# A few small products ahead of each pair of blocks in layer two

## The chip, the core and the metric

The kernel is one program on one core of a Trainium2 chip. The metric is device time in microseconds (us). Five engines have their own queues and run side by side: TensorE (PE, matrix products into PSUM, with the loading of weights shown apart as PEld), VectorE (DVE), ScalarE (ACT), GpSimd (POOL) and SyncE (SP, which issues the DMAs). They wait for one another through semaphores.

## What is computed

```python
def reference(**kwargs):
    attn_out = _attn_ref(**attn_kwargs)            # random-feature attention, 4 x 8 heads x 576 x 64
    x = attn_out.transpose(0, 2, 1, 3).reshape(B * S, H * D)     # 2304 tokens x 512
    x = _moe_ref(x=x, **moe_kwargs)                # layer one: h = x @ w_in; max(0.01 h, h) @ w_out
    return _moe2_ref(x=x, **moe2_kwargs)           # layer two, below

def _moe2_ref(x, w_in, w_out):                     # 512 -> 2048 -> 512
    h = x @ w_in
    relu6 = np.clip(h + 3.0, 0.0, 6.0)
    g = h * relu6 / 6.0
    return (g @ w_out).astype(np.float32)
```

All of it is in fp32. The change stands in the first product of layer two.

## The kernel before

**Number formats.** The large products of both layers hold each fp32 operand as two parts, high and low, of type fp32r, and make three products for one: high by high, low by high, high by low. One such product is one weight load and one matmul record in the trace. The products of the attention are plain fp32; each of them shows as two matmul records (the list of nine products in `K_unit` stands in the trace as 18 records of line L781). All records print "f32".

**Stages.** The 2304 tokens are cut into five groups of 512, 256, 512, 512 and 512 (`GN`). Attention for the next group runs between the products of layer one on the current group. Layer two follows, in the order of groups 0, 2, 3, 4, 1 (`ORDER2`); its first products already stand among the last of layer one.

**Layer two.** For a group of 512 tokens, `moe2` calls `Hpair(i)` for i = 0 to 7, one call for each pair of blocks of 128 hidden columns. It forms the pair's 2x2 block product by seven products of blocks (a Strassen form) instead of eight. `prod` issues one of the seven: six matmuls of 128x128 weights by 256 columns (line L1152, 42 matmuls a pair, 1344 in all for the 32 pairs of the four large groups). The results go into three regions: `R[0]` is the first half of PSUM bank `p`, `R[1]` and `R[2]` are the halves of bank `q`. The first product of a pair writes `R[0]` with `start` set at its first matmul, which clears it. The weights come by DMA into tiles (`fetch`, seen as `late_w<-in` or `third_w<-in`). Afterwards ACT and DVE make the activation, and `down` makes the output products (line L1057, also 128x256). The group of 256 tokens goes through `Hsingle`, which the change does not touch.

**Order.** A planner (`Graph.run`) lists all operations with costs and due times when the program is built, and writes each engine's queue in the order that it finds. A product's cost to the planner is the number in its `g.op(("pe", cost, mm))` call.

**Constants.** `ident` is a 128x128 identity, `ones` 128x128 of ones, both fp32; `zero` is 128x128 of zeros in fp32r. All are written once at the start of the program.

**Lines of the rows below.** L491 to L493 are the three products of `mm3` (layer one, 512 or 256 columns); L781 the product of keys and values in `K_unit`, 66 columns; L931 the transposes in `Q_unit`; L962 its numerator, with 64 stationary columns, written into either half of the PSUM partitions.

Of the kernel before, what the change touches and what calls it, by code (L numbers as in the profile page):

```python
# [325 lines left out]
def c_dve(n):  # L326
    return n / 0.96 + 69.0
# [6 lines left out]
def c_act(n, psum=False, ap=False):  # L334
    return n / 1.2 + (51.0 if psum else 93.0) + (93.0 if ap else 0.0)
# [6 lines left out]
def c_mm(n):  # L342
    return 114.0 if n == 256 else max(112.0, n / PACE)
# [7 lines left out]
def attn_moe_kernel(ctx: ExitStack, tc: tile.TileContext, qT, kT, qn, kn, v1, om2, w1i, w1o, w2i, w2o, out):  # L351
# [4 lines left out]
    nc = tc.nc  # L356
# [12 lines left out]
    def sb(name, shape, dt=F32, pool=const):  # L369
        return pool.tile(shape, dt, name=name)  # L370
# [91 lines left out]
    ident = sb("ident", [128, 128])  # L462
    wn = sb("wn", [128, 128])
    ones = sb("ones", [128, 128])
    zero = sb("zero", [128, 128], F32R)
# [4 lines left out]
    def Ps(use):  # L470
        return Buf("ps", use)


    def copy_alts(dst, src, n, psum=False):

        dve = ("dve", c_dve(n) if psum else c_dve2(n), lambda: nc.vector.tensor_copy(dst(), src()))
        return [("act", c_act(n, psum), lambda: nc.scalar.copy(dst(), src())), dve if psum else dve + (True,)]  # L477
# [9 lines left out]
    def two(b):  # L487
        return b.tiles[0].rearrange("p (k n) -> p k n", k=2)
# [154 lines left out]
    def fetch(b, kind, i, part, due, cols=slice(0, 512), to=0):  # L643
        d, done = late_w[kind, i, part]
        n = cols.stop - cols.start
        g.op([("sp", c_dma(128 * n * 8), lambda: nc.sync.dma_start(
            b.tiles[2].rearrange("p (h c) -> p h c", h=2)[:, :, to:to + n].bitcast(F32), d[:, :, cols].bitcast(F32)))],
             rd=[done, *ready.values()] if kind == "in" else [done], wr=[(b, to)], due=due)
        return b
# [464 lines left out]
    def moe2(grp, T):  # L1114
# [19 lines left out]
        def Hpair(i):  # L1134


            t0 = T + UP * i
            d = t0 - 8e3
            c = [Buf("w", line="c") for _ in range(4)]
            for k in range(4):  # L1140
                fetch(c[k], "in", i, k, d + UP * 0.1 * k, slice(0, 256) if k == 2 else slice(0, 512))
            p, q = Ps("H"), Ps("H")
            R = [lambda: p.tiles[0][:, 0:256], lambda: q.tiles[0][:, 0:256], lambda: q.tiles[0][:, 256:512]]
            bank = [(p, 0), (q, 0), (q, 1)]

            def prod(r, a, off, b, at, start):
                def mm():
                    for k in range(2):
                        w = [c[a].tiles[h][:, off + k * 128:off + k * 128 + 128] for h in range(2)]
                        m = [b.tiles[h][:, k * 256:k * 256 + 256] for h in range(2)]  # L1150
                        for n, (x, y) in enumerate(((0, 0), (1, 0), (0, 1))):
                            nc.tensor.matmul(R[r](), lhsT=w[x], rhs=m[y], start=start and k == n == 0, stop=k == 1 and n == 2,  # L1152
                                             skip_group_check=True)
                g.op([("pe", 6 * c_mm(256), mm)], rd=[c[a], b], wr=[bank[r]], due=t0 + UP * at, lag=APART if r == 0 and not start else 0.0)

            s, h0, h1 = Buf("u", line="s"), Buf("u", line="h"), Buf("u", line="h")
            hold = lambda i: s.tiles[0][:, i * 256:i * 256 + 256]

            def save(i, at):
                g.op(copy_alts(lambda: hold(i), R[0], 256, True), rd=[bank[0]], wr=[(s, i)], due=t0 + UP * at - 6e3)  # L1160

            def total(h, half, r, i, at):
                g.op([("dve", c_dve(256), lambda: nc.vector.tensor_tensor(  # L1163
                    out=h.tiles[0][:, half * 256:half * 256 + 256], in0=hold(i), in1=R[r](), op=ALU.add))],
                    rd=[bank[r], (s, i)], wr=[(h, half)], due=t0 + UP * at - 6e3)

            prod(0, 0, 0, B_["b11"], 0.0, True)
            prod(1, 0, 256, B_["b21"], 0.1, True)
            save(0, 0.1)
            prod(2, 1, 0, B_["t1"], 0.2, False)  # L1170
            total(h0, 0, 1, 0, 0.2)
            prod(0, 1, 256, B_["t2"], 0.3, False)
            save(1, 0.3)
            prod(0, 2, 0, B_["t3"], 0.5, False)
            save(0, 0.5)
            total(h1, 1, 2, 0, 0.5)
            prod(0, 3, 256, B_["t4"], 0.6, False)
            g.op(copy_alts(lambda: h1.tiles[0][:, 0:256], R[0], 256, True), rd=[bank[0]], wr=[(h1, 0)], due=t0 + UP * 0.7 - 6e3)
            prod(2, 3, 0, B_["b22"], 0.8, False)
            total(h0, 1, 2, 1, 0.8)  # L1180
            r, S, hb = Buf("xr", line="r"), Buf("xr", line="r"), Buf("hb")
            d = t0 + UP - 6e3
            for h, u, first, m in ((h1, p, 1, 1), (h0, q, 0, 3)):
                U, X = lambda u=u: u.tiles[0], lambda h=h: h.tiles[0]
                g.op([("act", c_act(512, False, True), lambda U=U, X=X: nc.scalar.activation(U(), X(), AF.Relu, bias=point5, scale=1.0 / 6.0))],  # L1185
                     rd=[h], wr=[u], due=d)
                for sub, to in enumerate((r, hb)):
                    view = lambda t, sub=sub: t.rearrange("p (t s c) -> p t s c", t=2, s=2)[:, :, sub]
                    place = lambda to=to, first=first, m=m: to.tiles[0].rearrange("p (b c) -> p b c", c=128)[:, first:first + m + 1:m]
                    g.op([("dve", c_dve(256), lambda U=U, X=X, view=view, place=place: nc.vector.scalar_tensor_tensor(  # L1190
                        out=place(), in0=view(U()), scalar=1.0, in1=view(X()), op0=ALU.min, op1=ALU.mult))],
                        rd=[u, h], wr=[(to, first)], also=[] if sub or first != 1 else [S], due=d)
            return r, S, hb, d, h0
# [32 lines left out]
        for i in range(NP + 1):  # L1226
            if i < NP:
                if fast:
                    r, S, hb, d, end_ = Hpair(i)
                    held_.append(hb)  # L1230
                    if i == NP - 1:
                        ahead = parts(held_[0], Buf("xr", line="S"), end - READY)
                    a, b = parts(r, S, T + UP * (i + 1 + LAG_A) - READY)
                else:
                    a, b = Hsingle(i)
                todo.append((i, a, b))
            if i:
                k, a, b = todo.pop(0)
                last = grp == ORDER2[-1] and k >= NP - 2
                down(acc, a, b, k, T + (UP if fast else UP * 0.5) * (k + 1 + LAG_A), [],  # L1240
                     T + UP * 0.5 * (NP + LAG_A) if last else None)
# [77 lines left out]
    for at, grp in enumerate(ORDER2):  # L1319
        n = GN[grp]  # L1320
        for k in () if grp in EARLYX else (0, 1, 3, 2):
            xr = Buf("xr")

            if n == 512:
                src, to, rd = x1[grp][k // 2][:, :, k % 2 * 256:k % 2 * 256 + 256], lambda xr=xr: two(xr), [x1d[grp, k // 2 * 2], x1d[grp, k // 2 * 2 + 1]]
            else:
                src, to, rd = x1[grp][k // 2][:, k % 2], lambda xr=xr, n=n: xr.tiles[0][:, :n], [x1d[grp, k]]
# [94 lines left out]
```

## Time and profile before

| | |
|---|---|
| median of 3 runs | 895.64 us (893.97 to 902.07) |
| the profiled execution's own time | 901.0 us |
| its span, first to last instruction | 898.9 us |
| PE busy | 886.6 us |
| granted PE clock | 1.000 over the span |
| DVE, ACT, POOL busy | 660.4, 480.1, 243.3 us |

The median is the time to compare with. The rows come from the profiled execution, which took 901.0 us; 2.1 us of that lie outside its span. A matmul's record covers its way through the array, so records of following matmuls overlap: what one matmul costs in a dense row is the distance from its start to the next one's start, and not its duration.

### The profile page before, as it was taken

The numbers are of one execution on the slowest core, as the hardware profiler recorded it, in microseconds if no ns is written. First come the engines' busy times: TensorE is split into PE (matmuls) and PEld (weight loads), VectorE is DVE, ScalarE is ACT, GpSimd is POOL, SyncE is SP. The second block draws the span as 40 slices with busy tenths as digits, with TensorE's granted clock in tenths as the row PEclk, the third lists the DMA queues.
The fourth block names the chain that finished last, engine by engine and source line by source line (L and its number), as shares of the span: only waits on it lengthen the run. The fifth ranks groups of instructions, "written<-read, shape, count | busy, mean of one in ns | idle before, by whom it ended". The sixth has DMA issues, their size and how long they took to land.

```text
span 898.9 us, 17816 instructions
## 1 busy us (share of the span) xinstructions
PE 886.6 (99%) x6338; PEld 792.3 (88%) x6338; DVE 660.4 (73%) x1663; ACT 480.1 (53%) x1127; POOL 243.3 (27%) x388
## 2 busy tenths in 40 slices
PE   8999999999999999999999999999999999999998
PEld 8888787799877777888888888999999999999998
DVE  6999778887888787565668446688678769867755
ACT  6976666675866555544554444544443445444443
POOL 2454446444546223010110001121112213222100
PEclk9999999999999999999999999999999999999999
DMA  9646544677467556988898349875786674587441
GB/s 331 188 158 213 177 156 133 202 235 224 118 222 250 165 165 186 334 308 315 290 351 328 132 153 286 287 258 182 264 309 215 232 249 151 199 279 233 128 152 51
DMA packets 91495, 197.99 MB, mean 220 GB/s; under 512 B 14736, under 2 KB 40976, under 8 KB 91408
## 3 DMA queue, kind: packets, MB, share of 16 engines
q1 hardware_dynamic: 91408, 196.87, 66.0%
q8 instruction: 50, 0.82, 0.4%
q14 instruction: 37, 0.30, 0.1%
HBM read 150.18 MB, written 46.66 MB: 219 GB/s over the span
## 4 chain that ended last, share of the span: by engine, by line
PE 91%; DVE 4%; DMA 3%; ACT 1%; POOL 1%; issue 0%; SPq 0%; DVEq 0%; POOLq 0%
PE bank L1057 19%; PE bank L1152 16%; PE bank L491 15%; PE bank L493 14%; PE bank L492 14%; PE bank L734 4%; PE bank L781 2%; PE bank L962 1%; DMA late_w<-in 1%; PE bank L803 1%; PE bank L931 1%; DVE junk L905 1%; DMA third_w<-in 1%; PE bank L857 1%; DMA first_xT<-qT 1%; DVE nm L699 1%
## 5 line engine op out<-in xcount | busy, mean ns | idle before, releaser
L477 ACT COPY late_u<-bank 128x256 f32<-128x256 f32 (+1 forms) x98 | 37.8, 385 | 112.5 <-PE bank L1152 95.4
L1057 PE MATMUL bank<-w,g 128*128 128x256 f32 x633 | 88.2, 279 | 1.3 <-ACT bank L1185 0.9
L999 DVE TENSOR_TENSOR g<-bank,g 128x512 fp32r<-128x512 f32 (+1 forms) x80 | 50.7, 634 | 51.0 <-ACT g L477 50.5
L997 ACT ACTIVATE bank<-bank 128x512 f32<-128x512 f32 (+1 forms) x80 | 44.1, 551 | 72.8 <-PE bank L493 72.4
L1057 PEld LDWEIGHTS bank<-w,g 128*128 128x128 f32 x633 | 79.6, 188 | 2.1 <-ACT bank L1185 1.1
L1152 PE MATMUL bank<-x,late_w 128*128 128x256 f32 x576 | 74.5, 278 | 1.3 <-DMA late_w<-in 1.2
L710 ACT ACTIVATE h<-bank,nm 128x128 f32<-128x128 f32 x228 | 63.7, 385 | 19.3 <-POOL nm L705 19.2
L1152 PEld LDWEIGHTS bank<-x,late_w 128*128 128x128 f32 x576 | 70.0, 188 | 1.7 <-DVE u L1163 1.4
L491 PE MATMUL bank<-g,w 128*128 128x512 f32 (+1 forms) x180 | 68.8, 382 | 1.2 <-ACT h L710 0.6
L491 PE MATMUL bank<-x,w 128*128 128x512 f32 (+1 forms) x180 | 69.1, 384 | 0.0
L493 PE MATMUL bank<-g,w 128*128 128x512 f32 (+1 forms) x180 | 66.3, 369 | 0.0
L493 PE MATMUL bank<-x,w 128*128 128x512 f32 (+1 forms) x180 | 66.3, 368 | 0.0
L492 PE MATMUL bank<-g,w 128*128 128x512 f32 (+1 forms) x180 | 66.1, 367 | 0.0
L492 PE MATMUL bank<-x,w 128*128 128x512 f32 (+1 forms) x180 | 66.1, 367 | 0.0
L699 DVE TENSOR_REDUCE nm<-bank 128x4 f32<-128x512 f32 (+2 forms) x76 | 47.1, 655 | 16.3 <-PE bank L734 14.6
L1057 PE MATMUL bank<-second_w,g 128*128 128x256 f32 x387 | 55.6, 278 | 0.0
L1152 PE MATMUL bank<-w,late_w 128*128 128x256 f32 x384 | 52.6, 279 | 0.2 <-DMA late_w<-in 0.2
L1057 PEld LDWEIGHTS bank<-second_w,g 128*128 128x128 f32 x387 | 49.6, 188 | 0.0
L1152 PEld LDWEIGHTS bank<-w,late_w 128*128 128x128 f32 x384 | 48.3, 189 | 0.6 <-DMA late_w<-in 0.4
L916 POOL TENSOR_TENSOR h<-h,den 128x512 f32<-128x512 f32 (+2 forms) x32 | 33.8, 1057 | 51.7 <-DVE den L911 33.4
L905 DVE CUSTOM_DVE_ANT_0 junk<-h,zr 128x128 bf16<-128x128 f32 (+1 forms) x128 | 46.0, 397 | 1.3 <-ACT zr L477 0.3
L491 PE MATMUL bank<-x,second_w 128*128 128x512 f32 (+1 forms) x120 | 45.4, 378 | 0.0
(371 smaller groups left out, 2404.0 us busy)
## 6 DMA issues: line engine op xcount, KB each, us to landing
late_w<-in SPq DMA_DIRECT2D x86, 512.0 KB, 4.6
in<-late_w SPq DMA_DIRECT2D x32, 512.0 KB, 3.8
late_w<-in SPq DMA_DIRECT2D x40, 256.0 KB, 4.6
third_w<-in SPq DMA_DIRECT2D x18, 512.0 KB, 4.6
wst<-w2i SPq DMA_DIRECT2D x16, 512.0 KB, 4.4
wst<-w2o SPq DMA_DIRECT2D x16, 512.0 KB, 4.2
x_t<-late_w SPq DMA_DIRECT2D x12, 512.0 KB, 4.8
v<-v SPq DMA_DIRECT2D x14, 330.0 KB, 4.6
```

What stands on the lines that cost most here:

```text
L477: return [("act", c_act(n, psum), lambda: nc.scalar.copy(dst(), src())), dve if psum else dve + (True,)]
L491: nc.tensor.matmul(o, lhsT=ah, rhs=bh, start=start, stop=False)
L492: nc.tensor.matmul(o, lhsT=al, rhs=bh, start=False, stop=False)
L493: nc.tensor.matmul(o, lhsT=ah, rhs=bl, start=False, stop=stop)
L699: g.op([("dve", c_dve(c * 128), lambda raw=raw, n_=n_: nc.vector.tensor_reduce(out=n_()[:, :, 0], in_=raw(), axis=AX.X, op=ALU.min))], rd= ...
L710: nc.scalar.activation(h.tiles[0][:, q * 128:q * 128 + 128], raw()[:, q], AF.Exp, bias=nm.tiles[0][:, q], scale=-1.0)
L734: nc.tensor.matmul(ps[bank].tiles[0][o, at:at + 128], lhsT=src.tiles[0][r, k * one + i * 128:k * one + i * 128 + n], rhs=wn[r], start=True ...
L905: nc.vector.tensor_tensor_reduce(out=jk.tiles[0][r, q % 2], in0=h.tiles[0][r, q * 128:q * 128 + 128], in1=zr[k].tiles[0][r, e], scale=1.0, ...
L997: g.op([("act", c_act(n, True), lambda: nc.scalar.activation(P(), P(), AF.Prelu, alpha=0.01))], wr=[p], due=d)
L999: g.op([("dve", c_dve(n), lambda: nc.vector.tensor_tensor(out=G1(), in0=P(), in1=G0().bitcast(F32), op=ALU.subtract))], rd=[p, (gg, 0)], w ...
L1057: nc.tensor.matmul(acc[bank].tiles[0][:, half * 256:half * 256 + 256], lhsT=src.tiles[x][:, q * 128:q * 128 + 128], rhs=w[k].tiles[y][:, c ...
L1152: nc.tensor.matmul(R[r](), lhsT=w[x], rhs=m[y], start=start and k == n == 0, stop=k == 1 and n == 2, skip_group_check=True)
```

## The change

`Hpair` gets a function `settle`, called at the head of the pair's first product. What it issues depends on `i % 4`: one plain fp32 product of 66 columns for 0, three of them for 1, two fp32r products of zeros of 66 columns for 2, and for 3 two plain fp32 products of 64 stationary by 256 moving columns, one for each half of the partitions. All write the region `R[0]` with `start` and `stop` set; the pair's first product then clears it. The planner's costs are as before.

```diff
+            def settle(to):
+                if i % 4 == 2:
+                    for _ in range(2):
+                        nc.tensor.matmul(to[:, 0:66], lhsT=zero, rhs=zero[:, 0:66], start=True, stop=True, skip_group_check=True)
+                elif i % 4 == 3:
+                    for e in range(2):
+                        nc.tensor.matmul(p.tiles[0][64 * e:64 * e + 64, 0:256], lhsT=ident[:, 0:64], rhs=ones[:, None, :].to_broadcast([128, 2, 128]),
+                                         start=True, stop=True, skip_group_check=True)
+                else:
+                    for _ in range(1 + 2 * (i % 4)):
+                        nc.tensor.matmul(to[:, 0:66], lhsT=ident, rhs=ones[:, 0:66], start=True, stop=True, skip_group_check=True)
+
             def prod(r, a, off, b, at, start):
                 def mm():
+                    if r == 0 and start:
+                        settle(R[0]())
                     for k in range(2):
```

The order of all other instructions is the same. PE's queue before, at the fifth pair (i = 4) of group 3 (`x_103` and `x_104` are blocks of the input, `late_w` is the fetched weights, `bank_178` is `p`; a bracket lists the semaphores of DMA queues or engines on which a row waits):

```order
L1152 MATMUL bank_177<-second_w_3_0_1057,late_w_0_0_3974 128x256 [waits DMAHW3_49,Activation_49]
L1152 MATMUL bank_177<-second_w_3_0_1057,late_w_0_0_3974 128x256 x5
L1152 MATMUL bank_178<-x_103,late_w_3_0_3977 128x256 [waits DMAHW5_49,DVE_49]
L1152 MATMUL bank_178<-x_103,late_w_3_0_3977 128x256 x5
L1152 MATMUL bank_179<-x_104,late_w_3_0_3977 128x256 [waits DVE_49]
L1152 MATMUL bank_179<-x_104,late_w_3_0_3977 128x256 x5
```

The same place in the changed kernel, where line L1152 has become L1166:

```order
L1166 MATMUL bank_177<-second_w_3_0_1057,late_w_0_0_3974 128x256 [waits DMAHW3_49,Activation_49]
L1166 MATMUL bank_177<-second_w_3_0_1057,late_w_0_0_3974 128x256 x5
L1156 MATMUL bank_178<-ones,ident 128x66 [waits DVE_49]
L1166 MATMUL bank_178<-x_103,late_w_3_0_3977 128x256 [waits DMAHW5_49]
L1166 MATMUL bank_178<-x_103,late_w_3_0_3977 128x256 x5
L1166 MATMUL bank_179<-x_104,late_w_3_0_3977 128x256 [waits DVE_49]
L1166 MATMUL bank_179<-x_104,late_w_3_0_3977 128x256 x5
```

One small product stands ahead of the pair's first six matmuls. It has taken over their wait for DVE, which frees the bank; the wait for the weights' DMA has stayed at the pair's own first matmul.

The last pair with i = 3, PE's queue of the changed kernel:

```order
L1166 MATMUL bank_181<-second_w_3_0_1057,late_w_1_0_3975 128x256 [waits DMAHW6_49,Activation_49]
L1166 MATMUL bank_181<-second_w_3_0_1057,late_w_1_0_3975 128x256 x5
L1152 MATMUL bank_178<-ones,ident 64x256 [waits DVE_49]
L1152 MATMUL bank_178<-ones,ident 64x256
L1166 MATMUL bank_178<-x_103,late_w_2_0_3976 128x256 [waits DMAHW0_49]
L1166 MATMUL bank_178<-x_103,late_w_2_0_3976 128x256 x5
```

Here two products, each into one half of the partitions, have come in ahead, and the wait for DVE stands at the first of them.

## Rows read from the trace of the kernel before

**Rows 1.** The page: span, busy time, granted clock in 40 slices.

```profile
span 898.9 us, 17816 instructions
PE 886.6 (99%) x6338; PEld 792.3 (88%) x6338; DVE 660.4 (73%) x1663; ACT 480.1 (53%) x1127; POOL 243.3 (27%) x388
PEclk9999999999999999999999999999999999999999
```

**Rows 2.** The waits of PE, 560 us to the end: total, times, longest.

```profile
PE bank L1152 <- DMA late_w<-in: 1.2, 1, 1.2
PE bank L1152 <- DMA third_w<-in: 0.5, 1, 0.5
PE bank L1057 <- DVE g L480: 0.2, 1, 0.2
```

**Rows 3.** Two stretches of 20 us in layer two: busy time and instructions by engine.

```profile
580.00:600.00 20.00, 20.00 (x172) 20.00 (x171) 16.15 (x39) 10.39 (x21) 4.55 (x7) 1.00 0.94 336
660.00:680.00 20.00, 20.00 (x179) 20.00 (x178) 15.94 (x43) 8.78 (x17) 1.42 (x4) 1.00 0.95 349
```

**Rows 4.** The chain that ended last, pieces of L1057: start, length, matmuls.

```profile
591.97 11.31 PE bank L1057 x96
...
670.62 10.88 PE bank L1057 x96
...
826.80 14.49 PE bank L1057 x123
```

**Rows 5.** PE's timeline, 67 us: start, length, line and tiles, records.

```profile
66.95 0.39 PE L493 MATMUL bank<-g,w 128*128 128x512 f32 x1
67.18 0.39 PE L781 MATMUL bank<-v,ht 128*128 128x132 f32 x2
67.40 1.90 PE L781 MATMUL bank<-v,h 128*128 128x66 f32 x16
69.10 0.48 PE L491 MATMUL bank<-g,w 128*128 128x512 f32 x1
69.42 0.40 PE L492 MATMUL bank<-g,w 128*128 128x512 f32 x1
```

**Rows 6.** PE's timeline, 176 to 178 us.

```profile
176.20 0.28 PE L493 MATMUL bank<-x,w 128*128 128x256 f32 x1
176.32 0.82 PE L931 MATMUL bank<-ident,h 128*128 128x128 f32 x6
176.89 0.36 PE L491 MATMUL bank<-x,w 128*128 128x256 f32 x1
177.09 0.28 PE L492 MATMUL bank<-x,w 128*128 128x256 f32 x1
...
177.56 0.28 PE L493 MATMUL bank<-x,w 128*128 128x256 f32 x1
```

**Rows 7.** PE's timeline, 179 to 181 us.

```profile
178.98 0.28 PE L493 MATMUL bank<-g,w 128*128 128x256 f32 x1
179.19 0.87 PE L962 MATMUL bank<-tq,kvf 128*64 128x384 f32 x4
179.98 0.38 PE L491 MATMUL bank<-x,w 128*128 128x256 f32 x1
180.21 0.28 PE L492 MATMUL bank<-x,w 128*128 128x256 f32 x1
...
180.56 0.28 PE L492 MATMUL bank<-x,w 128*128 128x256 f32 x1
...
180.90 0.28 PE L492 MATMUL bank<-x,w 128*128 128x256 f32 x1
```

**Rows 8.** PE's groups by shape: records, busy us, mean ns of one, idle us.

```profile
L962 PE MATMUL bank<-tq,kvf 128*64 128x384 f32 x16 | 3.5, 512 | 0.0
L962 PE MATMUL bank<-tq,kvf 128*64 128x192 f32 x16 | 1.7, 339 | 0.0
```

**Rows 9.** PE's timeline at two pairs' first products, 717.79 and 786.28 us.

```profile
717.79 1.39 PE L1152 MATMUL bank<-x,late_w 128*128 128x256 f32 x10 [1.21 <-DMA late_w<-in]
...
786.28 0.94 PE L1152 MATMUL bank<-x,late_w 128*128 128x256 f32 x6
```

## The prediction

> **What bounds the kernel now.** I read the page first. PE is busy for 886.6 of 898.9 us at the full granted clock (2.4 GHz) in every slice [rows 1], so the question is what the added products cost in PE's own row, and whether any of that falls into time in which PE waits. There is little such time: from 560 us to the end PE waits 1.9 us in all, three times [rows 2]. The other engines are at 73% and less and follow PE.
>
> The second view is PE's pace. In one stretch of 20 us in layer two PE has 172 records, in another 179, both with no idle time and the same clock [rows 3]. The chain gives the step exactly: 96 matmuls of 128x256 in 11.31 us are 117.8 ns each, 96 of the same line later in 10.88 us are 113.3 ns, and 123 later still in 14.49 us are 117.8 again [rows 4]. So the same matmul has a long and a short cadence, 4.5 ns or 3.9% apart. Going through the starts of all records of layer two, the cadence never changes inside a dense row: it is drawn anew only where the row is broken by a wait or by products of another kind, and then stays to the next break. The long one runs from 554.7 to 627.4 and from 786.3 to 862.5 us (148.9 us together), the short one from 627.4 to 785.9 nearly all the time and from 862.6 to the end. Turned wholly to the short one, the two long stretches would be 148.9 x 0.038 = 5.7 us shorter. Since the added products break the row 32 times, they also draw the cadence 32 times. That is a second term, of either sign, beside their cost.
>
> **What the change adds.** No product is moved, removed or given a new wait; DVE, ACT, POOL and SP keep their queues. The wait for the bank moves from the pair's first product to the small one ahead of it, and behind it stands the same product as before, so nobody waits longer for that. Each kind comes 8 times. A plain fp32 product is two records, an fp32r product one. The price of a break is the time from the start of the last large matmul ahead of it to the start of the second one behind it, less two ordinary steps; the second, because the first large matmul after a break is always held longer.
>
> Kind 0, one product of 66 columns, 128 stationary columns. The row of the same shape: 18 records of L781 start at 67.18 and the next large matmul at 69.10, so 0.107 us a record; that matmul then takes 69.42 - 69.10 = 0.32 us to the next start, where a 512-column step is about 0.23, so 0.09 more [rows 5]. Price: 2 x 0.107 + 0.09 = 0.30 us. The transposes of 128 columns agree: six records from 176.32 to 176.89, and 0.20 instead of 0.118 behind [rows 6], which is 0.65 us for six. Eight times 0.30: 2.4 us.
>
> Kind 1, three such products: 6 x 0.107 + 0.09 = 0.73 us, eight times 5.9 us.
>
> Kind 3, two products with 64 stationary and 256 moving columns, one to each half of the partitions. The nearest row is L962 with 384 columns and one pair of heads, also two products in four records: from 178.98 to 180.21 is 1.23 us, less two steps of 0.113 is 1.00 [rows 7]. The two halves run side by side, so there are two lengths of columns in a row. From 384 to 192 columns a record's mean falls from 512 to 339 ns [rows 8], which is 0.115 us for 128 columns; two lengths, each 128 columns shorter, give 1.00 - 0.23 = 0.77. By bare proportion it would be 0.67, and without any shortening 1.00; I take 0.77. Eight times: 6.2 us, between 5.4 and 8.0.
>
> Kind 2, two fp32r products of zeros, 66 columns. No row shows this type below 256 columns in layer two. Its floor is the share of columns, 66/256 of a step of 0.113, or 0.03 us each and 0.06 for both; its ceiling is kind 0's price for two records with a break, 0.30. The nearest row by shape is that of the 66-column records, 0.107 each [rows 5]; since the type does not change, I leave the 0.09 for the restart out: 0.21 us, eight times 1.7 us, between 0.5 and 2.4.
>
> Sum of the products: 2.4 + 5.9 + 6.2 + 1.7 = 16.2 us, between 14.2 and 18.7.
>
> What is hidden: at 717.79 the first product of a pair with i = 4, so with kind 0 ahead of it, waits 1.21 us for its weights [rows 9]. The small product ahead of it needs only constants and a free bank, so its 0.3 us falls into that wait. The pair at 786.28 has kind 3 ahead, with hardly a wait to fall into. I take 0.3 us off. If all later PE time were made up out of the two waits for weights it would be 1.7 us [rows 2], the bound.
>
> The cadence term. In the stretch where layer one has 256 columns (160 to 236 us), the breaks show how the draw goes. After plain fp32 products over the full array the long cadence followed in 6 of 8 breaks; the one at 176.32 is such a case, with four steps from 177.09 to 177.56 of 117.5 ns [rows 6]. After products of 64 stationary columns or 64 rows the short one followed in 10 of 13; the one at 179.19 is such a case, with three steps from 180.56 to 180.90 of 113 ns [rows 7]. So kinds 0 and 1 should leave PE in the long cadence and kind 3 in the short one; kind 2, with no change of type, I take to leave what it found. Placing the 32 first products by counting the 1344 records of L1152: kind 3 stands at about 554.7, 582.3, 630.9, 660.9, 708.3, 739.0, 786.3 and 816.7 us, kind 0 at 528, 563.9, 603.1, 639.1, 681.3, 717.8, 759.4 and 794.5. Stretches now short that would turn long: 627.4 to 630.9, 639.1 to 660.9, 681.3 to 708.3, 717.8 to 739.0 and 759.4 to 784.2, together 98.3 us, at 4.0% a loss of 3.9 us. Stretches now long that would turn short: 554.7 to 563.9, 582.3 to 603.1, 786.3 to 794.5 and 816.7 to 862.5, together 84.0 us, at 3.8% a gain of 3.2. Net +0.7 us. The ends: all short from the first settle on, -5.7; all long, the 158 us from 627.4 to 785.9 turned, +6.3.
>
> Against the profiled execution's own 901.0 us: 901.0 + 16.2 - 0.3 + 0.7 = 917.6. That execution lies 5.4 us above the median. If those 5.4 us are its 5.7 of long cadence, the changed kernel, which draws the cadence anew, does not inherit the difference and stays at 917.6; if they lie elsewhere, the same sum from the median is 912.2. I can't tell from one trace, and take a value between: 914.5 us.
>
> **The rivals.** First, the long cadence everywhere, since 24 of the 32 breaks are of full-array kinds: 901.0 + 15.9 + 6.3 = 923.2, from the median 917.8. For it speak the 6 of 8; against it the long stretches after kind 3 (some 143 of the 340 us of layer two).
>
> Second, the short cadence everywhere: 901.0 + 15.9 - 5.7 = 911.2, from the median 905.8. For it speak the waits inside layer two itself, after which the short one came in 7 of 11 breaks, and that a 66-column product may leave PE differently from one of 128 columns; against it the same 6 of 8.
>
> Third, on the other side: not slower. A small product would cost only its moving columns, because its weight load lies under the matmul before it and no restart is paid. Then a 66-column record takes 66/256 of 0.113, or 0.03 us, and kind 3's pairs two steps of 0.113: 0.06 + 0.18 + 0.06 + 0.23 = 0.53, eight times 4.2 us. With the short cadence throughout that is 901.0 + 4.2 - 0.3 - 5.7 = 899.2, from the median 893.8. It decides where a 66-column record costs 0.03 and not 0.11. The Trainium skill, page "TensorE: Matmul & The Clock Gate", section "Back-to-back issue gap", has a rule that speaks for it: the gap is the columns over 2.4 GHz plus 2.5 ns, 30 ns for 66 columns; by it the sum is about that of this rival. The row contradicts it: 66-column records with a new weight load each come 0.107 us apart, 18 in a row [rows 5]. Kind 2 is the only one that can still follow it.
>
> **How the numbers follow.** Forecast, the mix of cadences: 0.56, between 910 and 919. Long throughout: 0.17, 918 to 923. Short throughout: 0.19, 906 to 911, with the lower edge reaching 1% above the median. Not slower: 0.08, 893 to 904, mostly within 1% and 0.02 of it for faster by over 1%, which would need under 886.7. About 1% is what a measurement of this kernel can tell from no change: its three runs lie 0.9% apart. The range 906 to 921 leaves out the third rival and the upper part of the first. Slower by over 1% (above 904.6) holds the first, second and third of these four, the last of them but for 0.02: 0.90; within 1%: 0.08, from the short cadence's edge and the fourth; faster: 0.02.
>
> **What would show it.** In the changed kernel's trace, the two records of kind 0 should lie about 0.11 us apart with a first large matmul behind them of about 0.20 us; the six of kind 1 should take about 0.65; kind 3 should have its records side by side in pairs, about 0.26 us from pair to pair; kind 2's records should be 0.03 to 0.11 us apart. Behind kinds 0 and 1 the steps should be 117.8 ns, behind kind 3 113.3. The granted clock should stay at 1.00 and PE's waits at about 2 us. I am wrong if the 66-column records come 0.03 us apart, if the draw after full-array products is short, or if a late DMA or DVE stands ahead of the first products, which nothing in the queues suggests.

## The result, and the profile after

The changed kernel takes 908.7 us (median of 8 runs, 907.78 to 910.98); the kernel before, on the same chip, 898.51 us (8 runs, 893.97 to 902.99). The ratio is 1.0112, 95% interval 1.0081 to 1.0142: slower by 1.1%. The changed kernel's runs also lie closer together, within 3.2 us instead of 9.0. The profiled execution took 907.97 us, 7.0 more than that of before.

The page of the changed kernel, span and busy time of each engine, against [rows 1]:

```profile
span 905.8 us, 18019 instructions
PE 895.7 (99%) x6450; PEld 797.8 (88%) x6450; DVE 660.5 (73%) x1663; ACT 480.7 (53%) x1127; POOL 243.7 (27%) x388
```

PE has 112 records more (64 of L1156, 32 of L1152, 16 of L1149) and 9.1 us more of busy time; nothing changed on the other engines, and the granted clock stayed at full speed.

PE's timeline at the first dense pairs of each kind (start, length, line, records; a group of large matmuls is cut where the window ends):

```profile
564.40 0.62 PE L1166 MATMUL bank<-x,late_w 128*128 128x256 f32 x4
564.86 0.33 PE L1156 MATMUL bank<-ones,ident 128*128 128x66 f32 x2
565.00 0.48 PE L1166 MATMUL bank<-w,late_w 128*128 128x256 f32 x2
...
569.40 0.62 PE L1166 MATMUL bank<-second_w,late_w 128*128 128x256 f32 x4
569.86 0.78 PE L1156 MATMUL bank<-ones,ident 128*128 128x66 f32 x6
570.44 0.48 PE L1166 MATMUL bank<-w,late_w 128*128 128x256 f32 x2
...
576.55 0.62 PE L1166 MATMUL bank<-second_w,third_w 128*128 128x256 f32 x4
577.00 0.30 PE L1149 MATMUL bank<-zero 128*128 128x66 f32 x2
577.14 0.48 PE L1166 MATMUL bank<-w,late_w 128*128 128x256 f32 x2
...
583.25 0.62 PE L1166 MATMUL bank<-second_w,late_w 128*128 128x256 f32 x4
583.79 0.65 PE L1152 MATMUL bank<-ones,ident 128*64 128x256 f32 x4
584.37 0.50 PE L1166 MATMUL bank<-w,late_w 128*128 128x256 f32 x2
```

Each price reads off in the way of the prediction. Kind 0: from the fourth-last large matmul at 564.40 to the first behind at 565.00 are 0.60 us, and that one holds PE 0.20 us (two records end after 0.48, one alone takes 0.28); together 0.80, less five steps of 0.113, leaves 0.23. In the same way 0.67 for kind 1, 0.22 for kind 2 and 0.77 for kind 3. From the starts in nanoseconds, the same for each kind within 1 ns at the 29 places behind 553 us (the three ahead of it stand in a row of 512 columns or in the long cadence):

| kind | steps between the starts, ns | first large one behind | price | forecast |
|---|---|---|---|---|
| 0 | 115, 56, 81 | 201 | 0.226 us | 0.30 |
| 1 | 115, 56, 110, 112, 112, 111, 83 | 201 | 0.673 | 0.73 |
| 2 | 114, 29, 110 | 202 | 0.228 | 0.21 |
| 3 | 206, 7, 260, 7, 309 | 222 | 0.784 | 0.77 |

Eight of each make 15.3 us, where the forecast had 16.2.

The long pieces of L1057 in the chain that ended last, against [rows 4]:

```profile
593.83 10.88 PE bank L1057 x96
...
674.31 10.88 PE bank L1057 x96
...
834.95 13.94 PE bank L1057 x123
```

All are 113.3 ns a matmul. The first and the third of these pieces were at 117.8 before (11.31 and 14.49 us). From 554 us on, 47 large matmuls of the changed kernel (128x256, of all lines) are a long step of 117 to 120 ns from the next, single ones behind the breaks; in the profiled execution of before there were 1283. At 4.5 ns each that is 0.2 against 5.8 us.

PE's waits from 560 us to the end, against [rows 2]:

```profile
PE bank L1057 <- DVE g L480: 0.2, 1, 0.2
```

The two waits for weights, 1.7 us, are gone. So the 7.0 us between the two profiled executions are 15.3 for the products, less 5.6 for the cadence, less 1.7 for the waits, less 1.0 that these three do not name. The starts show what that is. Call a step of over 125 ns that is not beside a small product a held step: a wait or other late start, or the first matmul behind one. Behind 556 us the held steps of the large matmuls lie 4.3 us over 113.3 ns each before and 1.9 us now, so 0.7 us more is gone than the waits for weights; and a step of 0.43 us at 547.4 us, which the trace puts down in part to a wait for weights, is gone with 0.3 us.

### The profile page after: what moved, and what is told of

Its sections match the earlier page's. It is cut to its first block, busy times and chain, and to the rows that moved or that the text cites. A ratio compares the mean times of both kernels' runs of the same rounds, so it can differ in the third digit from the quotient of the medians.

```text
span 905.8 us, 18019 instructions
## 1 busy us (share of the span) xinstructions
PE 895.7 (99%) x6450; PEld 797.8 (88%) x6450; DVE 660.5 (73%) x1663; ACT 480.7 (53%) x1127; POOL 243.7 (27%) x388
## 4 chain that ended last, share of the span: by engine, by line
PE 92%; DVE 4%; DMA 1%; ACT 1%; POOL 1%; SPq 0%; issue 0%; DVEq 0%; POOLq 0%; ACTq 0%
PE bank L1057 19%; PE bank L1166 17%; PE bank L491 15%; PE bank L493 14%; PE bank L492 14%; PE bank L734 4%; PE bank L781 2%; PE bank L962 1%; PE bank L931 1%; PE bank L803 1%; DVE junk L905 1%; PE bank L1156 1%; DVE nm L699 1%; DMA out_raw<-wt 1%; DMA first_xT<-kT 1%; PE bank L857 1%
## 5 line engine op out<-in xcount | busy, mean ns | idle before, releaser
L1057 PE MATMUL bank<-w,g 128*128 128x256 f32 x633 | 87.1, 277 | 1.3 <-ACT bank L1199 0.9
L1057 PEld LDWEIGHTS bank<-w,g 128*128 128x128 f32 x633 | 78.6, 188 | 2.1 <-ACT bank L1199 1.1
L1166 PE MATMUL bank<-x,late_w 128*128 128x256 f32 x576 | 76.5, 281 | 0.0
L1166 PEld LDWEIGHTS bank<-x,late_w 128*128 128x128 f32 x576 | 69.8, 188 | 2.4 <-issue 2.3
L1057 PE MATMUL bank<-second_w,g 128*128 128x256 f32 x387 | 54.8, 276 | 0.0
L1166 PE MATMUL bank<-w,late_w 128*128 128x256 f32 x384 | 52.4, 279 | 0.0
L1057 PEld LDWEIGHTS bank<-second_w,g 128*128 128x128 f32 x387 | 48.9, 188 | 0.0
L1166 PEld LDWEIGHTS bank<-w,late_w 128*128 128x128 f32 x384 | 47.6, 188 | 0.9 <-issue 0.8
```

The source lines that it names most:

```text
L1057: nc.tensor.matmul(acc[bank].tiles[0][:, half * 256:half * 256 + 256], lhsT=src.tiles[x][:, q * 128:q * 128 + 128], rhs=w[k].tiles[y][:, c ...
```

## The experiments

What had to be told apart: why the long cadence is gone behind the small products (one kind that sets the short one, every break, or chance), and whether price and cadence together are all of the time. Each kernel but the last two is the changed one with another body of `settle`; the diffs show it. After each, the long steps of the profiled execution are counted as above; "rest" is its own time less the price of its small products (as its rows show it) and less 4.5 ns for each long step behind 554 us. A ratio is to the kernel before, run beside it: its medians were 900.09 us for the first four, 898.86 for the next four and 898.15 for the ninth.

**Kind 3 alone**

```diff
-                if i % 4 == 2:
...
+                if i % 4 == 3:
+                    for e in range(2):
+                        nc.tensor.matmul(p.tiles[0][64 * e:64 * e + 64, 0:256], lhsT=ident[:, 0:64], rhs=ones[:, None, :].to_broadcast([128, 2, 128]),
+                                         start=True, stop=True, skip_group_check=True)
```

> Only the pairs with i = 3 and 7 keep their small products (kind 3); kinds 0, 1 and 2 are gone. Price of the products: 8 x 0.784 = 6.3 us. Theory A (kind 3 sets the short cadence of 113.3 ns, the other kinds keep what they find): short from the first kind 3 at about 554 us on, except behind a wait that happens to set the long one, and then only to the next kind 3; time about 895.3 + 6.3 - 0.3 = 901 us, +0.3% on the median of before. Theory B (every break in layer two sets the short cadence): the same 901 us. Theory C (each break draws by chance): some of the 7 breaks after the first are followed by 117.8 ns for 10 to 45 us, 903 us or more.

900.48 us, ratio 1.0009 (0.9985 to 1.0032). The profiled execution: 901.72 us, price 6.3, 506 long steps. PE's timeline and the chain of this kernel around the second kind 3:

```profile
582.14 0.87 PE L1160 MATMUL bank<-second_w,late_w 128*128 128x256 f32 x6
582.94 0.65 PE L1149 MATMUL bank<-ones,ident 128*64 128x256 f32 x4
583.52 1.45 PE L1160 MATMUL bank<-w,late_w 128*128 128x256 f32 x10
```

```profile
593.33 11.31 PE bank L1057 x96
...
672.82 10.88 PE bank L1057 x96
```

A wait of 0.5 us at 568.6 had set the long cadence; the kind 3 at 582.9 found it and left it (96 matmuls in 11.31 us behind it, up to a wait at 628.7). So theory A, that kind 3 sets the short one, fell, and B, every break, with it; C was still open. The other kind 3 that found the long cadence, at 554.4, turned it.

**Kinds 0, 1 and 2 without kind 3**

```diff
-                elif i % 4 == 3:
-                    for e in range(2):
...
+                elif i % 4 < 2:
```

> Kinds 0, 1 and 2 stay, kind 3 is gone. Price: 8 x (0.226 + 0.673 + 0.228) = 9.0 us. Theory A: the long cadence that stands at about 550 us is carried through the small products, and changes only at a wait of PE; steps of 117.8 ns behind most of them until such a wait; time about 895.3 + 9.0 + 2 to 6 = 906 to 910 us. Theory B: 113.3 ns behind each of them from 555 us on; 904 us. Theory C: a mix that changes at single small products without a wait.

902.9 us, 1.0029 (1.0011 to 1.0048). Profiled 902.76 us, 281 long steps, most of them behind a wait at 866.7, past the last small product. The wait at 553 had set the short cadence, and all 21 breaks behind it left it short. The full-array kinds do not set the long one here, though the forecast had said that they would.

**Kind 2 at each pair**

```diff
+                for _ in range(2):
+                    nc.tensor.matmul(to[:, 0:66], lhsT=zero, rhs=zero[:, 0:66], start=True, stop=True, skip_group_check=True)
```

> Every pair gets kind 2 (two fp32r products of zeros, 66 columns): 32 x 0.228 = 7.3 us. Theory A: kind 2 keeps the cadence that it finds, long after about 550 us until a wait turns it; 905 to 908 us. Theory B: short behind each; 902.5 us. Theory C: a mix that changes at single places without a wait, about 905 us.

900.72 us, 1.0007 (0.9982 to 1.0032). Here the wait at 553 had set the long cadence (steps of 118, 117, 118, 118 ns), and the product at 555.2 turned it, while 28 others found the short one and left it: not chance, so C fell here. 43 long steps in all. The chain of this kernel:

```profile
592.20 10.88 PE bank L1057 x96
...
670.63 10.88 PE bank L1057 x96
...
827.39 13.94 PE bank L1057 x123
```

With a price of 7.3 us the time is that of before within 0.3%: what the products cost, the cadence gave back.

**One matmul of zeros with the full 256 columns at each pair**

```diff
+                nc.tensor.matmul(to[:, 0:256], lhsT=zero, rhs=zero[:, None, :].to_broadcast([128, 2, 128]), start=True, stop=True, skip_group_check=True)
```

> Every pair gets one fp32r product of zeros with the full 256 columns, a matmul like those around it, so the row is lengthened but not broken: 32 x 0.113 = 3.6 us. All theories that lay the cadence to breaks expect no redraw: the cadence changes at waits of PE alone, long and short stretches as in the kernel before, time 895.3 + 3.6 + 0 to 6 = 899 to 905 us. If any added instruction at the head of a pair set the short cadence, it would be 113.3 ns throughout and 899 us, with no stretch of 117.8 ns behind it.

898.56 us, 0.9978 (0.9956 to 1.0). Price 0.124 us each, 4.0 in all, and 77 long steps. I had expected no redraw, and was wrong: the two that found the long cadence, at 538.7 and 784.55 us, turned it within six matmuls. Where such a product finds the short one, its steps show that it does break the row a little: 119 ns to the next start, then 119, 124, 118 and 113.

**Kind 0 at each pair**

```diff
+                nc.tensor.matmul(to[:, 0:66], lhsT=ident, rhs=ones[:, 0:66], start=True, stop=True, skip_group_check=True)
```

> Every pair gets kind 0 (one plain fp32 product of 66 columns): 32 x 0.226 = 7.2 us. Theory D, formed after the first four runs (a small product keeps the cadence that it finds; only waits of PE and the mixed stretch with layer one set it): the products at about 538 and 546 us find the long cadence and leave it long, all that find the short one leave it short; about 900 to 903 us by what the waits set. Theory A' (a full-array plain fp32 product sets the long cadence in 6 of 8 cases, as its breaks in layer one did): long behind most, 908 us.

900.66 us, 1.0026 (1.0004 to 1.0048). The two at 538 and 546 us, in the stretch mixed with layer one, left the long cadence as theory D has it. But the one at 554.5 found it (117, 118, 118, 118, 120) and turned it within six matmuls, so D does not hold behind 554. The 28 others found the short one and left it. Theory A' fell.

**The same with 128 columns**

```diff
+                nc.tensor.matmul(to[:, 0:128], lhsT=ident, rhs=ones, start=True, stop=True, skip_group_check=True)
```

> As the run before, but the product has 128 moving columns, like the transposes of layer one from which the forecast took its draw. Price by those rows: two records 0.11 us apart, the last 0.03, and 0.09 for the restart, 0.23 us, 32 x 0.23 = 7.4 us. Theory D': the number of columns made the difference; 128 columns set the long cadence where they found the short one, behind most of the 32, and 66 don't: 907 to 909 us. Theory D without it: the cadence stays as found, 900 to 903 us as with 66 columns.

900.49 us, 1.0029 (1.0009 to 1.005). The price is that of kind 0 to the nanosecond (115, 108, 29, then 201), so 66 columns save nothing over 128. D' fell as well: 27 breaks found the short cadence and left it, and both that found the long one behind 553 us (554.6 and 646.1 us) turned it. The number of columns is not what made layer one's breaks draw otherwise.

**The product of zeros at two pairs of a group**

```diff
+                if i in (3, 5):
+                    nc.tensor.matmul(to[:, 0:256], lhsT=zero, rhs=zero[:, None, :].to_broadcast([128, 2, 128]), start=True, stop=True, skip_group_check=True)
```

> One fp32r product of zeros with 256 columns at the pairs with i = 3 and 5 alone: 8 x 0.124 = 1.0 us. In the fourth run such a product turned the long cadence into the short one both times that it found it. If that holds: the long cadence lasts from a wait to the next such product at most, time 895.3 + 1.0 = 896 us, 0.3 to 0.4% under the median of before, and less spread. If those two were chance: long stretches of 70 us as in before, 899 us and the ratio 1.00.

896.96 us, 0.9987 (0.9964 to 1.001), 0.2% under before and inside the noise. It spread from 892.87 to 901.46, no less than before; 286 long steps in the profiled execution, most of them behind 856 us, past the last such product. The same product at each pair, above, did as well (0.9978, an interval that overlaps this one).

**The pair's own first matmul twice**

```diff
+                nc.tensor.matmul(to, lhsT=c[0].tiles[0][:, 0:128], rhs=B_["b11"].tiles[0][:, 0:256], start=True, stop=True, skip_group_check=True)
```

> Every pair issues its own first matmul twice, with the pair's weights and columns, the second one clearing what the first left: a matmul like all others, 32 x 0.113 = 3.6 us. If the product of zeros turned the cadence by its operands (a constant, the same 128 columns read twice), this one turns nothing: 0.113 us each, no changed step around it, cadence set by waits alone, 899 to 904 us. If any further matmul at this place does it, the long cadence ends at the first one behind each wait, 899 us.

899.27 us, 1.0003 (0.9981 to 1.0025). The added matmul stands in the row like its neighbours, 0.113 us. The long cadence that a wait at 640.1 set was carried through six of them, to the wait at 706.1; one more, at 581.6, found it and turned it, but with a late start behind it (steps of 120 and 154 ns). Another, at 574.7, was held by late starts too (196 and 192 ns), found the short cadence, and the long one followed. From its chain:

```profile
591.12 10.88 PE bank L1057 x96
...
670.35 11.31 PE bank L1057 x96
```

So a further matmul that keeps the row's regular step does not end the long cadence; those that ended it broke the step. That a break is enough does not follow: the kind 3 at 582.9 us broke it too and left the long one.

**Kind 1 at each pair**

```diff
+                for _ in range(3):
+                    nc.tensor.matmul(to[:, 0:66], lhsT=ident, rhs=ones[:, 0:66], start=True, stop=True, skip_group_check=True)
```

> Every pair gets kind 1 (three plain fp32 products of 66 columns), the dearest of the full-array kinds: 32 x 0.673 = 21.5 us, more than all of the change. If the time is a sum of three terms (a base of about 892.5 us that the profiled executions of all runs so far leave when the rest is taken off, the price of the small products as their rows show it, and 4.5 ns for each matmul in the long cadence), it is 892.5 + 21.5 + 0 to 1.5 = 914 to 915.5 us. If part of the price is hidden beside other work and only small prices showed in full, it is under 912 us. If dense breaks bring the long cadence, it is 918 us or more.

915.03 us, 1.020 (1.0176 to 1.0224); profiled 913.73. The time is in the 914 to 915.5 us of the sum. The cadence is short behind 554 us but for single steps behind the breaks and for 13 matmuls behind a late start (188 ns) at 796.6, which the product at 798.5 ended:

```profile
594.91 10.88 PE bank L1057 x96
...
676.97 10.88 PE bank L1057 x96
...
840.83 13.94 PE bank L1057 x123
```

**The kernel before, twice more**

> The kernel before, unchanged, to see another execution of it. If its spread of some 9 us between runs is the draw of the cadence and of waits behind 554 us, this one shows other stretches of 117.8 ns than the first, and its time less 4.5 ns for each matmul in the long cadence and less its waits behind 554 us with their restarts is again about 892 to 893 us. If the spread has another source, that remainder differs by several us.

897.25 us, with long steps from 554.5 to 581.7 and from 780.7 to 858.7, 893 in all. Its chain:

```profile
591.87 10.88 PE bank L1057 x96
...
823.02 14.49 PE bank L1057 x123
```

> The kernel before once more, with the same expectations: other stretches of the long cadence, and the same remainder of 892 to 893 us; or a remainder several us away, if the spread has another source.

900.38 us, with the long cadence from 713.7 to 784.0 and again nearly throughout behind 784.7, 1496 long steps:

```profile
591.11 10.88 PE bank L1057 x96
...
745.92 10.95 PE bank L1057 x93
...
825.12 14.49 PE bank L1057 x123
```

The same program has its long stretches at other places in each execution. Its waits for weights behind 560 us were 0.3 and 0.2 us here, not 1.7. From 580 to 600 us PE has 172 records in [rows 3] and 179 in the last repetition, at the same granted clock and DMA shares of 0.94 and 0.91, so neither the instructions of a stretch nor its share of traffic decides the cadence. The expected remainder came out: beyond the 1.9 us that the changed kernel has of them, the held steps of the three executions are 2.4, 0.6 and 0.8 us, and their rests in the table below, less these, are 892.8, 892.6 and 892.8.

**All profiled executions together**

| kernel | own time | price | long steps | at 4.5 ns | rest |
|---|---|---|---|---|---|
| before | 901.0 | 0 | 1283 | 5.8 | 895.2 |
| before, again | 897.25 | 0 | 893 | 4.0 | 893.2 |
| before, again | 900.38 | 0 | 1496 | 6.7 | 893.6 |
| changed | 907.97 | 15.3 | 47 | 0.2 | 892.5 |
| kind 3 alone | 901.72 | 6.3 | 506 | 2.3 | 893.2 |
| without kind 3 | 902.76 | 9.0 | 281 | 1.3 | 892.5 |
| kind 2 at each | 900.31 | 7.3 | 43 | 0.2 | 892.8 |
| zeros, 256 columns | 897.11 | 4.0 | 77 | 0.3 | 892.8 |
| kind 0 at each | 900.29 | 7.2 | 56 | 0.3 | 892.8 |
| 128 columns | 902.11 | 7.2 | 342 | 1.5 | 893.3 |
| zeros at two pairs | 895.43 | 1.0 | 286 | 1.3 | 893.2 |
| first matmul twice | 899.77 | 3.6 | 616 | 2.8 | 893.4 |
| kind 1 at each | 913.73 | 21.5 | 66 | 0.3 | 891.9 |

The own times span 18 us, the rests 3.3, and without the first execution of before, which had 1.7 us of waits for weights, 1.7. Less its held steps behind 556 us as well (1.8 to 4.3 us), each of the thirteen comes to 890.1 to 891.0 us. So the price, the cadence and the waits with their restarts are all but 1 us of what differs between these executions.

## Why the prediction was right, and where not

**PE's row as the place of the cost: right.** The price shows nearly in full. A part hidden beside other work would show as a smaller rest. Kind 1 at each pair, with 21.5 us of price, has the smallest (891.9), but only 0.6 to 1.5 us under those of the other kernels with small products, so no more than that is hidden; a late start at 547 us, 0.2 to 0.3 us over the cadence in the executions of before, is gone there and is some of it. The third rival, products that cost their moving columns alone, is out: two records with 66 columns cost 0.226 us with their restart, and only the first of kind 2's two comes near the 0.03 us (0.029, the second 0.110).

**The prices: right in sum, 15.3 for 16.2.** Kinds 0 and 1 were taken 0.06 to 0.07 us too high, because they were priced with 107 ns for each record, the mean of the 18 in [rows 5]. That row too has steps of 111 and 112 ns, but one of 58, and a last one of 83; in a break of two records the short ones are all there is (56 and 81 ns). Kind 3's extrapolation from 384 columns and kind 2, for which there was no row, held to 0.02 us.

**The cadence: the step that failed.** The step "kinds 0 and 1 should leave PE in the long cadence" gave a net +0.7 us; the changed kernel has the short one behind every small product from 554 us on, which against the profiled execution is -5.6. That is the second rival, for which the text gave 905.8 to 911.2 us; the measured 908.7 lies in the middle of it, under the forecast's own 910 to 919 but inside the range. Against the profiled execution the forecast's sum was 917.6, and 907.97 came out: of the 9.6 us too many, 0.9 are the price, 6.3 the cadence and 2.4 the waits. That 914.5 missed the median by less, 5.8 us, is owed to the value taken between the two bases, and that 908.7 is in the range to the room left for the second rival.

The draw of layer one's breaks was the wrong row to take: over all runs, behind 553 us, 199 of 199 small products that found the short cadence left it short, with 66, 128 or 256 columns, fp32 or fp32r. Of 8 that found the long one 7 turned it. (The doubled matmul is not counted in either.) This holds for that stretch alone: ahead of it, at about 538 and 546 us, where layer one's products stand between, 12 of 13 small products that found the long cadence left it long, two of them in the changed kernel, as the forecast would have had it for kinds 1 and 2. In the executions without a product there, the long cadence found at that place (553 us in before and once in its repetitions) ran on until the next wait. So behind 553 us the small products do something for layer two that the kernel before leaves to its waits. It would explain why its runs lie 9 us apart and the changed kernel's 3, but that isn't shown: only single executions were traced, and with the product of zeros at each pair, 77 long steps in the traced one, the runs still lay 6.4 us apart.

**The waits: mis-sized, and not the change's.** 0.3 us were taken off for a wait of 1.21 us; both waits for weights vanished. But in the two repetitions of before they were only 0.3 and 0.2 us, with no product to hide them. Most of the 1.7 us for weights in [rows 2] was that execution's.

**The base: rightly left open.** The three executions of before had 5.8, 4.0 and 6.7 us of long cadence, 5.5 on the mean. By price and cadence the change is 15.3 - (5.5 - 0.2) = 10.0 us; measured on the medians, 908.7 - 898.5 = 10.2. That these agree so well is in part luck: the mean of the three own times, 899.5, is 1.0 us over the median of before, and 907.97 is 0.7 under that of the changed kernel. Between the profiled executions the change is 8.4 us, and the other 1.6 us are held steps, the one at 547 us among them.

What stays open is why a break sets the one cadence or the other. The sequence of steps behind it differs by a nanosecond or two (201, 120, 117, 115 goes short; 201, 119, 117, 118 goes long), which the records name but do not explain. Nor is it shown why layer one's breaks found the short cadence and set the long one, which none did behind 553 us; nor why the small products at 538 and 546 us left the long one; whether the operands of layer one matter for it was not tried.

## What to carry to other kernels

Where one engine's row is dense, read the start-to-start step of its commonest instruction over the whole span before any sum is made: a step with two values is a term of its own, here 4 to 7 us in 900, and in three executions of one kernel it differed by 2.7 us, more than the waits did (1.7). An instruction put into this dense row cost its full step and the restart behind it, so that the small products at 32 pairs cost as much as 135 large ones (15.3 us at 0.113), and what they may repair must be worth that. A cheaper repair was one ordinary matmul of zeros at each pair, at 0.124 us instead of 0.48 on the mean, which made the sum 0.2% smaller instead of 1.1% larger, at the edge of what can be told.

## What the runs showed of the hardware that was not expected

The same matmul of 128x256 in fp32r has two steps at the same granted clock, 113.3 and 117.8 ns, each kept for hundreds of matmuls and across changes of operands (246 and more in a row). It changed only at an interruption, a wait or a product that broke the row's step, and not at each: 199 small products left the short one as it was. A plain fp32 product of 66 columns over the full array costs as much as one of 128 columns, 0.226 us with its restart. A product of zeros with 256 columns takes 0.124 us in a row of 0.113, and disturbs three more steps behind it; the same matmul as its neighbours, doubled, takes 0.113 and disturbs none.
